# Late query projections inside the pair visit, one PSUM bank for the first product, and matmuls on zeros at the start

## The chip, the cores and the metric

The kernel runs on one core of a Trainium2 chip. The metric is the device time of one execution in microseconds (us). The kernel before takes 1054.83 us, the median of three runs (1054.11 to 1055.69).

## What is computed

Two stages follow each other. The first is linear attention over 8 batches and 8 heads (576 tokens, head dimension 64) with a feature map of 2 x 128 features; the second is a two-layer network with a squared Relu over all 4608 tokens (512 to 2048 to 512).

```python
def phi(x):
    proj = np.einsum('bhsd,df->bhsf', x, w_phi)
    proj = proj - np.max(np.abs(proj), axis=-1, keepdims=True)
    return np.concatenate([np.exp(proj), np.exp(-proj)], axis=-1)
q_p, k_p = (phi(q), phi(k))
kv = np.einsum('bhsf,bhsd->bhfd', k_p, v)
z = np.sum(k_p, axis=2)
num = np.einsum('bhsf,bhfd->bhsd', q_p, kv)
den = np.einsum('bhsf,bhf->bhs', q_p, z)[..., None] + 1e-06
attn = num / den            # heads are joined to tokens of 512 values
g = np.maximum(attn @ w_in, 0.0) ** 2
out = g @ w_out
```

## The kernel before

**Attention** goes by pairs of heads, 32 in all. The first six (`early`, L646) run step by step while the weights of the second stage are fetched and prepared. The other 26 are late pairs, and most of their matmuls stand in a *visit* (`visit`, L837): one TensorE step that holds, in this order, the key projections of pair i+1 (`k_main`, L579, in row halves of the array, and `k_tail`, L585, in column halves), the value products of pair i (L635, L640) and the numerators of pair i-1 (L853), both in column halves. The query projection of pair i is a step of its own in `late` (L920 to L926): four matmuls of 288 columns, two per head, in row halves. Its results go from three PSUM tiles to the tile `pt` by three copies (L927 to L931), and from there through a reduction over partitions on POOL (L936), a subtraction and two exponentials to the numerators of the next visit and to the denominators.

**The second stage** (`moe`, L984) goes by chunks of 256 tokens (18) and groups of 256 hidden units (8), 144 units in all. A *first product* (`gemm1`, L1002) is 24 matmuls of 256 columns into one tile `ph`; its result is split on the way to the *second product* (`gemm2`, L1032, 12 matmuls of 512 columns): Relu into `r` (L1011), its square in two precisions, `gh` (L1013) and back into `ph` (L1015), and their difference `gl` (L1018, recorded at L306).

**PSUM** has eight banks: `pp` two, `pn` and `pv` one each, `ph` two buffers of one bank, `po` two. In the first five pairs `ph` also holds the query projections (L689) and `po` the key projections.

**The order** of all instructions is written by a planner in the kernel file (`Plan.order`, L151). Each step has engines it may run on, an expected time, the steps it follows, the buffers it uses and a rank; the planner goes through time and gives each free engine the ready step of the lowest rank. Between steps of different array tilings (`mode`) it adds CHANGE to TensorE's time and prefers to stay in a tiling (STAY). The ranks of the steps up to about rank 70 come from a long string, RANKS. The order is fixed when the kernel is built; on the chip each engine takes its instructions in that order.

```python
o = P.add("PE", 1.0, q_proj, [q_load[p]], [("q", p)] + pq, R(RQ), mode=ROWS)          # L926
v = P.add("PE", us, work, after, use, rank, mode=(ROWS if k is not None else COLS, COLS))   # L871
```

Of the kernel before, what the change touches and what calls it, by code (L numbers as in the profile page):

```python
# [52 lines left out]
CHANGE = 0.15  # L53
RA, RQ, RZ = 1.3, 0.4, 0.3
COLD = 1.1
# [23 lines left out]
class Plan:  # L79
# [71 lines left out]
    def order(self):  # L151
# [36 lines left out]
        while done < len(self.ops):  # L188
# [28 lines left out]
            op.start, op.end = t, t + us * (COLD if e == "PE" and t < 125.0 else 1.0)  # L217
# [75 lines left out]
def tile_kernel(ctx, tc, qp, kp, vp, w_phi, w_in, w_out, out):  # L293
# [72 lines left out]
    ph_ = tiles(ps, "ph", [128, 2, T], F32, 2)  # L366
# [8 lines left out]
    make_identity(nc, ident)  # L375
    V.memset(ones, 1.0)
# [13 lines left out]
    def power(src, dst, top, after, uses, rank, k=1):  # L390
# [21 lines left out]
        return P.add("DVE", 0.7 + 0.16 * k, bits, [a], key + [("pn", ("pw", n))], rank)  # L412

# [104 lines left out]
    def value_in(f, n, rank, joined, pw):  # L518
# [5 lines left out]
                      for E_, us, E, lk in (("DVE", 0.64, V, 4.0), ("POOL", 1.15, G, 0.0))])  # L524
# [121 lines left out]
    def early(p):  # L646
# [42 lines left out]
        q_to = lambda h: flat(ph_[2 * p + h]) if free else pp_["qt", p][:, h, :]  # L689
        q_use = [("ph", 2 * p + h) if free else ("pp", ("qt", p)) for h in range(2)]  # L690
# [144 lines left out]
    N0 = 320  # L835

    def visit(i):  # L837
        n, s, k = (x if EARLY <= x < NPAIR else None for x in (i - 1, i, i + 1))
        rank = PER_PAIR * i + RA
        pp, pn, pv = ("pp", ("a", i)), ("pn", ("a", i)), ("pv", ("a", i))  # L840

        def work():
            if k is not None:
                k_main(k, lambda h: pp_["a", i][:, h, :])
                k_tail(k, pn_["a", i][:, N0:N0 + 128])
            if s is not None:
                kv_main(s, pv_["a", i])
                kv_tail(s, pv_["a", i])
            if n is not None:
                for to, lo, hi in ((pn_["a", i][:, 0:N0], 0, N0), (pv_["a", i][:, 256:256 + S - N0], N0, S)):  # L850
                    for s_ in range(2):
                        for h in range(2):
                            PE.matmul(out=to[64 * h:64 * h + 64, :], lhsT=kz_[n][:, 128 * s_ + 64 * h:128 * s_ + 64 * h + 64],  # L853
                                      rhs=qe_[2 * n + h].rearrange("p (s x) -> p s x", s=2)[:, s_, lo:hi],
                                      start=s_ == 0, stop=s_ == 1)

        us, after, use = 0.1, [], [pn, pv]
        if k is not None:
            loads(k, rank - 4.0)
            us += 1.24  # L860
            after += [k_load[k]]
            use += [pp, ("k", k)]
        if s is not None:
            us += 2.15
            after += exps[s] + [exp_t[s], v_load[s]]
            use += kv_use(s)
        if n is not None:
            us += 1.93
            after += [kz_of[n]] + qexp[n]
            use += [("kz", n), ("qe", 2 * n), ("qe", 2 * n + 1)]  # L870
        v = P.add("PE", us, work, after, use, rank, mode=(ROWS if k is not None else COLS, COLS))  # L871
        nums = []
        if n is not None:
            for bank, key, x, lo, hi in ((pn_, pn, 0, 0, N0), (pv_, pv, 256, N0, S)):
                first, second = copy(hi - lo, lambda lo=lo, hi=hi: n_[n][:, lo:hi],
                                     lambda bank=bank, x=x, lo=lo, hi=hi: bank["a", i][:, x:x + hi - lo])
                nums.append(P.add(*first, [v], [key, ("n", n)], rank + 0.1, other=[second]))
        if s is not None:
            turn(s, v, pv, lambda: pv_["a", i][:, 0:256], rank + 0.1)
        if k is not None:  # L880
            keys(k, v, lambda h: pp_["a", i][:, h, :], [pp, pp], v, lambda: pn_["a", i][:, N0:N0 + 128], pn, rank + 0.2)
        if n is not None:
            tokens(n, nums, rank + 0.4)
# [14 lines left out]
    def late(p):  # L898
# [17 lines left out]
        zc = P.add("DVE", 1.75, column, [o], [("z4", p), ("za", p), ("zr", p), ("zc", p)], R(RZ), lock=4.0)  # L916
        pq = [("pp", ("Q", p)), ("pn", ("Q", p)), ("pv", ("Q", p))]
        rest = lambda h: (pn_, pv_)[h]["Q", p][:, 0:SH]

        def q_proj():  # L920
            for lo in (0, SH):
                for h in range(2):
                    PE.matmul(out=rest(h) if lo else pp_["Q", p][:, h, 0:SH], lhsT=wst[64 * h:64 * h + 64, :],  # L923
                              rhs=q_[p][64 * h:64 * h + 64, lo:lo + SH], start=True, stop=True)

        o = P.add("PE", 1.0, q_proj, [q_load[p]], [("q", p)] + pq, R(RQ), mode=ROWS)  # L926
        first, second = copy(2 * SH, lambda: pt_[p][:, :, 0:SH], lambda: pp_["Q", p][:, :, 0:SH])  # L927
        pt = [P.add(*first, [o], [pq[0], ("pt", p)], R(RQ + 0.1), other=[second])]
        for h in range(2):
            first, second = copy(SH, lambda h=h: pt_[p][:, h, SH:S], lambda h=h: rest(h))  # L930
            pt.append(P.add(*first, [o], [pq[1 + h], ("pt", p)], R(RQ + 0.1), other=[second]))  # L931
        qexp[p], dens = [], []
        for h in range(2):
# [4 lines left out]
                [pt[0], pt[1 + h], pool_next], [("pt", p), ("mx", n)], R(RQ + 0.2), lock=0.0)  # L938
# [45 lines left out]
    def moe(c, f, w_done):  # L984
        n = c * NFP + f
        m, bank = LEAD + n, n + 2 * BANKS
# [20 lines left out]
        if f:  # L1007
# [4 lines left out]
            out=r_[n], in_=ph_[bank], func=AF.Relu, scale=cw[:, f, 0:1]), [g1], [("ph", bank), ("r", n)], Q)  # L1012
        sq = P.add("ACT", act_us(512), lambda: A.activation(out=gh_[n], in_=r_[n], func=AF.Square),  # L1013
                   [o], [("r", n), ("gh", n)], Q)
        o = P.add("ACT", 0.59, lambda: A.activation(out=ph_[bank], in_=r_[n], func=AF.Square),  # L1015
                  [o], [("ph", bank), ("r", n)], Q, other=[("DVE", 0.76, lambda: V.scalar_tensor_tensor(
                      out=ph_[bank], in0=ph_[bank], scalar=cw[:, f, 0:1], in1=r_[n], op0=ALU.mult, op1=ALU.mult), None)])
        o = P.add("DVE", 0.70, lambda: sub(V, gl_[n], ph_[bank], gh_[n].bitcast(F32)),  # L1018
                  [o, sq], [("ph", bank), ("gh", n), ("gl", n)], Q)
# [15 lines left out]
        g2 = P.add("PE", 2.74, gemm2, [o] + list(w_done[f, False]),  # L1035
# [93 lines left out]
    "ACD]1k>%<ELlWgVP]lB._^StESJfL=[CY1ITMeI#4rABQDZ$UqY(KKZeKGZnL{PDPuM2OLG#M&E$Z8LYVwTQJYT.?SO_MMe0ND?a"  # L1129
    "N@WsXNNtERMlHBMtHkO6L*ZtGSHYJHNhR-W<B>HtLuQ@KqViKUHdM<J1B5S3OMU>Q/Qe]DJwJ?Qy_1AgGsR{Z^AVU}RgU-7fI_B3"  # L1130
    "D7P=NZBcA!7HV=Ny@bHWO[K0E$W1D/JrFc:,RXC*_xV<]|NEUk?2S,DyP`;?SsLM@d@mQQGBJ@K8E0QFQ)AJM#g@L=>OUOMbHzJj"
    "J@NOM6M=SbPIOQJ#>pKC6iKzIMDSLtJOH,KJ:UQ#ORVXAjVOM&SLV$4YTFDoC8>KNI>>GoE0Wm@HA)JOK/QX?*[sXqIYE2EfLr^1"
    "TXTIA4A=fIF1DDPXPk/dOjK=W|L=AfM:EKC=<ADTH/EHDrJ[A.IEQJCeS+<.WPVuL;GJX0ZeNvOsEhJ?Q;J*E)LlK?KqGnE=G=^/"
    "D{LQ:3EN?pPT_C1QNZ<QTdEG;QOzD)P8=RM^ASM3MbHoa=HMNnG.7oD|Q7^JVBL}T5QpNJMKBnGGNEE.2G@PX<LHIYH!P(Q4B%=O"
# [50 lines left out]
```

## Time and profile before

| What | Value |
|---|---|
| median of 3 runs | 1054.83 us |
| the profiled execution | 1055.12 us |
| its span, first to last instruction | 1053.3 us |
| mean granted TensorE clock | 0.994 of 2.4 GHz |
| instructions | 19429 |
| busy: TensorE (PE) / VectorE (DVE) / ScalarE (ACT) / GpSimd (POOL) | 1025.4 / 718.4 / 620.4 / 164.6 us |
| HBM read and written | 59.18 and 12.99 MB |

All rows come from one profiled execution; its times count from the span's start. PE is TensorE's matmuls, PEld its weight loads, which overlap them. The matmuls are pipelined and a row's duration runs into the next row, so the time that a step takes on TensorE is read from its start to the start of what follows. An engine's idle time stands in brackets behind a row, with what released it.

### The profile page before, as it was taken

Reading aid. Unit: us, or ns where it says so; the run is one execution under the profiler, and the core shown is the slowest. Engines: PE = TensorE matmul, PEld = TensorE weight load, DVE = VectorE, ACT = ScalarE, POOL = GpSimd, SP = SyncE. Lnnn points to the kernel's source line nnn. Section 1 sums busy time; section 2 is a strip of 40 time slices with the busy share of each in tenths; the row PEclk is TensorE's granted clock in tenths of the full one; section 3 lists DMA queues with packets and bytes.
Section 4 is the critical chain, followed back from the end, with each engine's and each line's share of the span. In section 5 each row is a group of like instructions: output and inputs, shape, how many; then the busy total and the mean of one; then the engine's idle time right before and its main releaser. Section 6 shows DMA issues by size and latency. Waiting matters only on the chain.

```text
span 1053.3 us, 19429 instructions
## 1 busy us (share of the span) xinstructions
PE 1025.4 (97%) x7678; PEld 706.6 (67%) x7762; DVE 718.4 (68%) x1526; ACT 620.4 (59%) x1117; POOL 164.6 (16%) x86
## 2 busy tenths in 40 slices
PE   8869999999999999999999999999999999999998
PEld 6545766667767666666676666676666666677775
DVE  5877688887897887878787767787687775111111
ACT  7896875666665555666666655566555555333333
POOL 2532411111110111111111011111110111000000
PEclk9998999999999999999999999999999999999999
DMA  9834222212222120222221221122121101000000
GB/s 356 299 122 148 100 68 77 77 47 68 77 58 74 50 72 20 74 58 77 58 77 58 57 78 44 41 55 73 45 65 27 45 16 43 1 21 21 1 21 21
DMA packets 66143, 73.47 MB, mean 70 GB/s; under 512 B 35204, under 2 KB 44036, under 8 KB 64004
## 3 DMA queue, kind: packets, MB, share of 16 engines
q1 hardware_dynamic: 66052, 72.22, 21.8%
q8 instruction: 61, 1.00, 0.4%
q14 instruction: 30, 0.25, 0.1%
HBM read 59.18 MB, written 12.99 MB: 69 GB/s over the span
## 4 chain that ended last, share of the span: by engine, by line
PE 93%; DMA 3%; ACT 2%; DVE 1%; issue 1%; SPq 0%; ACTq 0%; DVEq 0%
PE po L1032 37%; PE ph L1002 36%; PE pv L635 5%; PE pp L579 3%; PE pn L853 3%; PE pv L853 2%; PE pp L923 2%; DMA raw0o<-in_w_out_dram 1%; PE pn L923 1%; PE pv L640 1%; PE pn L585 1%; DMA k<-in_kp_dram 1%; PE pv L749 1%; PE pn L398 0%; PE pp L730 0%
## 5 line engine op out<-in xcount | busy, mean ns | idle before, releaser
L1002 PE MATMUL ph<-ring,win 128*128 128x256 f16 x3456 | 400.6, 273 | 0.0
L1002 PEld LDWEIGHTS <-win 128*128 128x128 f16 x3456 | 336.3, 98 | 72.0 <-issue 10.2
L1011 ACT ACTIVATE r<-ph,cw 128x512 f32<-128x512 f32 x144 | 99.1, 688 | 248.1 <-PE ph L1002 247.7
L306 DVE TENSOR_TENSOR gl<-ph,gh 128x512 bf16<-128x512 f32 x144 | 98.9, 686 | 183.9 <-ACT ph L1015 178.1
L936 POOL PARTITION_ALL_REDUCE mx<-pt x52 | 114.3, 2198 | 635.7 <-ACT pt L310 420.0
L1032 PE MATMUL po<-wh,gh 128*128 128x512 f32 x576 | 172.5, 420 | 0.0
L1032 PE MATMUL po<-wl,gl 128*128 128x512 bf16 x560 | 147.0, 379 | 0.8
L1032 PE MATMUL po<-wl,gh 128*128 128x512 bf16 x508 | 135.1, 381 | 4.6
L1032 PEld LDWEIGHTS po<-wh,gh 128*128 128x128 f32 x576 | 99.0, 189 | 29.1 <-issue 9.8
L1032 PEld LDWEIGHTS <-gl 128*128 128x128 bf16 x576 | 56.3, 98 | 68.0
L1013 ACT ACTIVATE gh<-r 128x512 fp32r<-128x512 f32 x144 | 90.9, 631 | 5.8 <-PE po L1032 1.6
L1032 PEld LDWEIGHTS <-gh 128*128 128x128 bf16 x576 | 44.8, 98 | 73.5 <-issue 39.8
L1015 ACT ACTIVATE ph<-r 128x512 f32<-128x512 f32 x144 | 84.4, 586 | 0.5
L635 PE MATMUL pv<-e,v 128*64 128x256 f32 x512 | 63.5, 391 | 0.6 <-ACT kz L310 0.4
L310 ACT ACTIVATE n<-pn 128x320 f32<-128x320 f32 (+1 forms) x32 | 13.8, 431 | 77.4 <-PE pn L853 77.1
L950 DVE SCALAR_TENSOR_TENSOR pt<-qe,zc,pt 128x576 f32<-128x576 f32 x52 | 42.3, 816 | 19.3 <-ACT pt L948 18.8
L306 DVE TENSOR_TENSOR qe<-pt,mx 128x576 f32<-128x576 f32 x52 | 39.0, 750 | 17.1 <-POOL mx L936 16.8
L601 ACT ACTIVATE e<-e 128x512 f32<-128x512 f32 x64 | 39.8, 622 | 17.2 <-DVE e L598 17.2
L941 ACT ACTIVATE qe<-qe 128x576 f32<-128x576 f32 x52 | 35.1, 675 | 22.4 <-DVE qe L306 22.4
L635 PEld LDWEIGHTS pv<-e,v 128*64 128x64 f32 x512 | 37.2, 141 | 16.3 <-issue 2.3
L887 DVE STREAM_TRANSPOSE kvs<-pv 128x256 f32<-128x256 f32 x26 | 11.5, 444 | 48.8 <-PE pv L853 44.6
L948 ACT ACTIVATE pt<-qe,zc 128x576 f32<-128x576 f32 x52 | 40.2, 775 | 3.9
(188 smaller groups left out, 1281.2 us busy)
## 6 DMA issues: line engine op xcount, KB each, us to landing
v<-in_vp_dram SPq DMA_DIRECT2D x32, 320.0 KB
k<-in_kp_dram SPq DMA_DIRECT2D x32, 288.0 KB
q<-in_qp_dram SPq DMA_DIRECT2D x32, 288.0 KB
rb<-rd SPq DMA_DIRECT2D x64, 144.0 KB
out_dram<-o SPq DMA_DIRECT2D x34, 256.0 KB
td<-kvs SPq DMA_DIRECT2D x26, 128.0 KB
kz<-td SPq DMA_DIRECT2D x104, 32.0 KB
raw0i<-in_w_in_dram SPq DMA_DIRECT2D x1, 1024.0 KB
```

Source lines behind the costliest of these rows:

```text
L306: eng.tensor_tensor(out=out_, in0=a, in1=b_, op=ALU.subtract)
L601: o = P.add("ACT", act_us(512), lambda n=n: A.activation(out=e_[n][:, :, 1, :], in_=e_[n][:, :, 0, :], func=AF.Exp, scale=-1.0), [o], [("e ...
L635: PE.matmul(out=to[64 * h:64 * h + 64, 0:256], lhsT=v_[p][:, t, h, :], rhs=e_[2 * p + h][:, t].rearrange("p s f -> p (s f)"), start=t == 0 ...
L853: PE.matmul(out=to[64 * h:64 * h + 64, :], lhsT=kz_[n][:, 128 * s_ + 64 * h:128 * s_ + 64 * h + 64], rhs=qe_[2 * n + h].rearrange("p (s x) ...
L936: o = P.add("POOL", par_us(S), lambda n=n, h=h: G.partition_all_reduce(mx_[n], pt_[p][:, h, :], channels=128, reduce_op=bass_isa.ReduceOp. ...
L948: o = P.add("ACT", act_us(S, 1), lambda h=h, qe=qe, y=y: A.activation(out=y(), in_=qe(0), func=AF.Copy, scale=zc_[p][:, 2 * h:2 * h + 1]), ...
L950: o = P.add("DVE", 0.82, lambda h=h, qe=qe, y=y: V.scalar_tensor_tensor(out=y(), in0=qe(1), scalar=zc_[p][:, 2 * h + 1:2 * h + 2], in1=y() ...
L1002: PE.matmul(out=ph[:, j, :], lhsT=win[w][:, t, 128 * ff:128 * ff + 128], rhs=ring[half][x][:, t, c0:c0 + T], start=k == 0, stop=k == 3 * K ...
L1011: o = P.add("ACT", act_us(512, 1), lambda: A.activation(out=r_[n], in_=ph_[bank], func=AF.Relu, scale=cw[:, f, 0:1]), [g1], [("ph", bank), ...
L1013: sq = P.add("ACT", act_us(512), lambda: A.activation(out=gh_[n], in_=r_[n], func=AF.Square), [o], [("r", n), ("gh", n)], Q)
L1015: o = P.add("ACT", 0.59, lambda: A.activation(out=ph_[bank], in_=r_[n], func=AF.Square), [o], [("ph", bank), ("r", n)], Q, other=[("DVE", ...
L1032: PE.matmul(out=po_[po[i][1]], lhsT=g[:, j, 128 * i:128 * i + 128], rhs=w[:, j, :], start=(ff == 0 and s == 0), stop=(ff == 2 * NFP - 1 an ...
```

## The change

- The query projection of a late pair is no step of its own any more. The visit has three steps: *rows* (512 columns of both heads' query projections into `pn` and `pv`, then the keys), *columns* (the last 64 query columns, the keys' tail, the value products, all into a new one-bank tile `pz`) and *numerators* into `pn` and `pv`, which wait for the copies of the query projections out of these banks. The copies are of 512, 512 and 2 x 64 columns.
- `ph` has one buffer instead of two; its bank goes to `pz`. In the first five pairs the query projections use `ph` and `pz`.
- r squared is kept in `r` in SBUF. The second square runs in place behind `gh` on ScalarE or VectorE, and `gl` reads `r` and `gh`. The Relu may also run on VectorE.
- At the start TensorE runs eight matmuls of 512 columns on a tile of zeros.
- The scaling of the input weights may no longer run on POOL.
- The planner's numbers: CHANGE is 0.18 instead of 0.15, a slower TensorE ahead of 125 us is no longer assumed, a step that holds a single bank already is not released by that bank's last use, and RANKS is another string.

```diff
-CHANGE = 0.15
+CHANGE = 0.18
-COLD = 1.1
+WARM = 8
...
-            least = max([open_at.get(tag, 0.0) for tag, n in alone(op)] + [a.start + 0.001 for a in op.behind], default=0.0)
+            least = max([open_at.get(tag, 0.0) for tag, n in alone(op) if holder.get(tag) != n] + [a.start + 0.001 for a in op.behind], default=0.0)
...
+    pz_ = tiles(ps, "pz", [128, 512], F32, 1, None)
-    ph_ = tiles(ps, "ph", [128, 2, T], F32, 2)
+    ph_ = tiles(ps, "ph", [128, 2, T], F32, 1)
...
+    warmer = o_[0].bitcast(BF16)[:, 0:512]
+    V.memset(warmer, 0.0)
...
+    def warm():
+        for _ in range(WARM):
+            PE.matmul(out=pn_["warm", 0], lhsT=warmer[:, 0:128], rhs=warmer, start=True, stop=True)
+    P.add("PE", 3.2, warm, [], [("pn", ("warm", 0))], -100.0)
...
-                      for E_, us, E, lk in (("DVE", 0.64, V, 4.0), ("POOL", 1.15, G, 0.0))])
+                      for E_, us, E, lk in (("DVE", 0.64, V, 4.0),)])
...
+        def rows():
+            if s is not None:
+                for h in range(2):
+                    PE.matmul(out=(pn_, pv_)[h]["Q", i], lhsT=wst[64 * h:64 * h + 64, :], rhs=q_[s][64 * h:64 * h + 64, 0:512],
+                              start=True, stop=True)
             if k is not None:
                 k_main(k, lambda h: pp_["a", i][:, h, :])
...
+        def columns():
+            for h in range(2 if s is not None else 0):
+                for c in range(0, 128, 64):
+                    PE.matmul(out=pz_["a", i][c:c + 64, 64 * h:64 * h + 64], lhsT=wbf[:, 128 * h + c:128 * h + c + 64],
+                              rhs=q_[s][:, 512:576], start=True, stop=True)
+            if k is not None:
+                k_tail(k, pz_["a", i][:, 128:256])
             if s is not None:
+                kv_main(s, pz_["a", i][:, 256:512])
+                kv_tail(s, pz_["a", i][:, 256:512])
...
+            v = P.add("PE", us_r, rows, need, use_r, R(0.0), mode=ROWS)
+            c = P.add("PE", us_c, columns, need + [v], use_c, R(0.0), mode=COLS)
...
+            v3 = P.add("PE", 1.94, numerators, need + [c] + pt_of.get(s, [])[:2], use_n, R(0.0), mode=COLS)
...
-        o = P.add("PE", 1.0, q_proj, [q_load[p]], [("q", p)] + pq, R(RQ), mode=ROWS)
...
-        o = P.add("ACT", 0.59, lambda: A.activation(out=ph_[bank], in_=r_[n], func=AF.Square),
-                  [o], [("ph", bank), ("r", n)], Q, other=[("DVE", 0.76, lambda: V.scalar_tensor_tensor(
...
-        o = P.add("DVE", 0.70, lambda: sub(V, gl_[n], ph_[bank], gh_[n].bitcast(F32)),
-                  [o, sq], [("ph", bank), ("gh", n), ("gl", n)], Q)
+        o = P.add("ACT", act_us(512), lambda: A.activation(out=r_[n], in_=r_[n], func=AF.Square),
+                  [sq], [("r", n)], Q, other=[("DVE", 0.70, lambda: V.tensor_tensor(
+                      out=r_[n], in0=r_[n], in1=r_[n], op=ALU.mult), 4.0)])
+        o = P.add("DVE", 0.70, lambda: sub(V, gl_[n], r_[n], gh_[n].bitcast(F32)),
+                  [o, sq], [("r", n), ("gh", n), ("gl", n)], Q, lock=4.0)
```

## Rows read from the trace of the kernel before

**Rows 1.** The page's first part: busy us, share of the span, instructions.
```profile
PE 1025.4 (97%) x7678; PEld 706.6 (67%) x7762; DVE 718.4 (68%) x1526; ACT 620.4 (59%) x1117; POOL 164.6 (16%) x86
```

**Rows 2.** Stretches: busy us of PE, PEld, DVE, ACT, POOL; granted clock, DMA, GB/s.
```profile
0.00:125.00 125.00, 106.03 (x1071) 74.12 (x1074) 90.84 (x162) 101.58 (x178) 45.41 (x33) 0.96 0.60 216
...
50.00:75.00 25.00, 20.92 (x256) 13.28 (x254) 19.57 (x39) 23.70 (x42) 9.83 (x5) 1.00 0.45 138
500.00:600.00 100.00, 99.35 (x733) 67.80 (x742) 78.17 (x174) 61.49 (x114) 12.85 (x6) 1.00 0.23 64
```

**Rows 3.** TensorE's time line around one query projection: start us, us, instruction.
```profile
480.91 2.78 PE L1002 MATMUL ph<-ring,win 128*128 128x256 f16 x24
483.62 0.76 PE L923 MATMUL pp<-q,wraw 64*128 64x288 f32 x4
...
484.79 1.20 PE L1032 MATMUL po<-wh,gh 128*128 128x512 f32 x4
...
487.57 2.78 PE L1002 MATMUL ph<-ring,win 128*128 128x256 f16 x24
490.11 1.18 PE L1032 MATMUL po<-wh,gh 128*128 128x512 f32 x4
...
492.86 0.39 PE L398 MATMUL pn<-ident,m 128*128 128x128 f32 x2
```

**Rows 4.** TensorE's time line through one visit.
```profile
501.10 1.16 PE L579 MATMUL pp<-wraw,k 64*128 64x128 f32 x16
502.19 0.44 PE L585 MATMUL pn<-wraw,k 128*64 128x128 f32 x4
502.46 1.90 PE L635 MATMUL pv<-e,v 128*64 128x256 f32 x16
504.18 0.60 PE L640 MATMUL pv<-et,v 128*64 128x256 f32 x4
504.61 1.25 PE L853 MATMUL pn<-qe,kz 128*64 128x320 f32 x8
...
506.65 1.20 PE L1032 MATMUL po<-wh,gh 128*128 128x512 f32 x4
```

**Rows 5.** The time lines of ScalarE and VectorE during that visit.
```profile
501.20 0.69 ACT L1011 ACTIVATE r<-ph,cw 128x512 f32<-128x512 f32 x1 [1.98 <-PE ph L1002]
501.92 0.63 ACT L1013 ACTIVATE gh<-r 128x512 fp32r<-128x512 f32 x1
502.46 0.58 ACT L1015 ACTIVATE ph<-r 128x512 f32<-128x512 f32 x1
...
503.68 0.64 DVE L306 TENSOR_TENSOR gl<-ph,gh 128x512 bf16<-128x512 f32 x1
```

**Rows 6.** Single lines of the kernel: duration in ns, shortest, median and longest.
```profile
L617 DVE TENSOR_TENSOR ez<-e x52: 635/688/1660, 135.1 to 844.8; 128x512 f32<-128x512 f32 x52
...
L306 DVE TENSOR_TENSOR gl<-ph,gh x144: 640/692/693, 100.2 to 1046.2; 128x512 bf16<-128x512 f32 x144
...
L936 POOL PARTITION_ALL_REDUCE mx<-pt x52: 2141/2142/2689, 143.8 to 877.8; - x52
...
L310 ACT ACTIVATE pt<-pp x26: 628/632/652, 142.7 to 873.7; 128x576 f32<-128x576 f32 x26
```

**Rows 7.** The head: TensorE's time line, and the stretch from 79 to 86 us.
```profile
4.18 0.69 PE L585 MATMUL pn<-wraw,k 128*64 128x128 f32 x4 [4.18 <-DMA k<-in_kp_dram]
4.80 2.08 PE L579 MATMUL po<-wraw,k 64*128 64x128 f32 x16
...
35.25 1.16 PE L579 MATMUL po<-wraw,k 64*128 64x128 f32 x16 [1.84 <-DMA k<-in_kp_dram]
...
79.30 1.09 PE L730 MATMUL pp<-ident,pt 128*128 128x128 f32 x4 [4.88 <-DVE e L598]
...
80.84 3.68 PE L635 MATMUL pv<-e,v 128*64 128x256 f32 x16 [0.16 <-ACT n L310]
...
79.00:86.00 7.00, 6.54 (x30) 3.94 (x32) 5.11 (x7) 5.61 (x10) 2.02 (x1) 0.51 0.43 148
```

More of the change, by code (lines that the diff above doesn't have):

```diff
@@ L216, in order @@
             us, _, lock = op.ways[e]
-            op.start, op.end = t, t + us * (COLD if e == "PE" and t < 125.0 else 1.0)
+            op.start, op.end = t, t + us
             if lock is not None:
@@ L835, in tile_kernel @@
     N0 = 320
+    pt_of = {}
     def visit(i):
@@ new lines, in numerators @@
+        def numerators():
+            for to, lo, hi in ((pn_["n", i][:, 0:N0], 0, N0), (pv_["n", i][:, 0:S - N0], N0, S)):
+                for s_ in range(2):
+                    for h in range(2):
+                        PE.matmul(out=to[64 * h:64 * h + 64, :], lhsT=kz_[n][:, 128 * s_ + 64 * h:128 * s_ + 64 * h + 64],
+                                  rhs=qe_[2 * n + h].rearrange("p (s x) -> p s x", s=2)[:, s_, lo:hi],
+                                  start=s_ == 0, stop=s_ == 1)
+        us_r, us_c, need, use_r, use_c, use_n = 0.0, 0.0, [], [pz], [pz], [pn, pv]
@@ L858, in visit @@
         if k is not None:
             loads(k, rank - 4.0)
-            us += 1.24
-            after += [k_load[k]]
-            use += [pp, ("k", k)]
-        if s is not None:
-            us += 2.15
-            after += exps[s] + [exp_t[s], v_load[s]]
-            use += kv_use(s)
-        if n is not None:
[L868 to L871, printed above, removed]
+            us_r += 0.9
@@ new lines, in visit @@
+        if us_r:
+            v = P.add("PE", us_r, rows, need, use_r, R(0.0), mode=ROWS)
+            c = P.add("PE", us_c, columns, need + [v], use_c, R(0.0), mode=COLS)
+        if s is not None:
+            pt_of[s] = []
+            for h, (to, key) in enumerate(((pn_, qn), (pv_, qv))):
+                first, second = copy(512, lambda h=h: pt_[s][:, h, 0:512], lambda to=to: to["Q", i])
+                pt_of[s].append(P.add(*first, [v], [key, ("pt", s)], R(0.05), other=[second]))
+            first, second = copy(128, lambda: pt_[s][:, :, 512:576],
+                                 lambda: pz_["a", i][:, 0:128].rearrange("p (h x) -> p h x", h=2))
+            pt_of[s].append(P.add(*first, [c], [pz, ("pt", s)], R(0.05), other=[second]))
@@ L872, in visit @@
         nums = []
         if n is not None:
-            for bank, key, x, lo, hi in ((pn_, pn, 0, 0, N0), (pv_, pv, 256, N0, S)):
+            v3 = P.add("PE", 1.94, numerators, need + [c] + pt_of.get(s, [])[:2], use_n, R(0.0), mode=COLS)
+            for bank, key, lo, hi in ((pn_, pn, 0, N0), (pv_, pv, N0, S)):
                 first, second = copy(hi - lo, lambda lo=lo, hi=hi: n_[n][:, lo:hi],
-                                     lambda bank=bank, x=x, lo=lo, hi=hi: bank["a", i][:, x:x + hi - lo])
-                nums.append(P.add(*first, [v], [key, ("n", n)], rank + 0.1, other=[second]))
+                                     lambda bank=bank, lo=lo, hi=hi: bank["n", i][:, 0:hi - lo])
+                nums.append(P.add(*first, [v3], [key, ("n", n)], R(0.1), other=[second]))
@@ L914, in column @@
                 V.tensor_copy(out=zc_[p][32 * b:32 * b + 32, :], in_=zr_[p].rearrange("p (j b) -> p b j", b=4)[:, b, :])
[L916 to L924, printed above, removed]
-        o = P.add("PE", 1.0, q_proj, [q_load[p]], [("q", p)] + pq, R(RQ), mode=ROWS)
[L927 to L931, printed above, removed]
+        zc = P.add("DVE", 1.8, column, [o], [("z4", p), ("za", p), ("zr", p), ("zc", p)], R(RZ), lock=4.0)
+        pt = pt_of[p]
         qexp[p], dens = [], []
@@ L985, in moe @@
         n = c * NFP + f
-        m, bank = LEAD + n, n + 2 * BANKS
+        m, bank = LEAD + n, n + BANKS
         half, c0 = divmod(c * T % RING, HR)
@@ L1128 @@
 RANKS = (
[L1129 to L1133, printed above, removed]
```

87 lines of the change are left out of this document (48 added, 39 removed).

## The prediction, made before the kernel with the change was run

> **What bounds the kernel now.** I read the page's engine table first, then three stretches, then TensorE's own time line. TensorE is busy for 97% of the span, and in the steady part for more: 99.35 of 100 us between 500 and 600, against 78 on VectorE and 61 on ScalarE [rows 1, 2]. There a microsecond of TensorE work is a microsecond of the run, and an instruction elsewhere is free until its queue is late. The first 125 us are of another kind: TensorE idles 19 of them, and from 50 to 75 ScalarE is the fuller engine with 23.70 of 25 [rows 2]. So the steady part is costed by TensorE's columns, the head by what its waits could give back.
>
> **The unit of the steady part** is a first product and a second product. From 487.57 to 490.11 a first product takes 2.54 us, from there to 492.86 a second one 2.75, together 5.29 [rows 3]. What lies between such pairs is attention.
>
> **What is removed: the query projection as a step of its own.** There are 26 late pairs, each with its projection at line 923, and every one has products on both sides: 14 times a first product ahead and a second behind, 12 times another order. From 480.91 to 487.57 (first product, projection, second product) 6.66 us go by where 5.29 would without it: 1.37 us [rows 3]. The projection itself is 1.17 of that (483.62 to 484.79), the other 0.20 is what its neighbours lose by the change of tiling. The 12 in another order lie between 1.17 and 1.37; one neighbour pays in each, so 1.30. Weighted, 1.34 us per pair are removed, 34.8 in all.
>
> **What is added to the visit.** The row half holds 512 columns per head, both heads at once on the two row halves, in two passes, as every float32 matmul here. The price of a column comes from the value products: eight instructions of 256 columns per column half last from 502.46 to 504.18, 0.215 each [rows 4]. So 512 columns last 0.43 and two passes 0.86. The visit opens in this tiling anyway, for the keys, so no change of tiling comes with it. The column half holds the last 64 columns: four instructions per column half (two heads, two passes), 0.21 by columns alone. But short instructions cost more than their columns: the keys' 16, eight per row half, last from 501.10 to 502.19, 0.136 each for 128 columns worth 0.107, and line 585's, two per column half, last 0.27 [rows 4]. If 0.136 is a floor per instruction, four cost 0.54. The nearest reading is 0.03 on top of the columns, so 4 x (0.053 + 0.03) = 0.33; I take that and keep 0.21 and 0.54 as ends. Added: 0.86 + 0.33 = 1.19. Net 1.34 - 1.19 = 0.15 per pair, times 26 **3.9 us gained**. The ends: 1.34 - 1.07 gives 7.0 gained, 1.30 - 1.40 gives 2.6 lost.
>
> **The new wait inside the visit.** The numerators now write the two banks that the projection filled, and so wait for two copies of 512 columns, each under the 0.632 of the copy of 576 [rows 6]. The projection's matmuls end 0.9 us after the visit opens. ScalarE is then busy with the Relu and the two squares of the product before, until 503.04, 1.94 after the opening [rows 5]; with two copies behind that it is 3.2. Meanwhile TensorE has the keys, the 64 columns, the keys' tail and the value products: 0.86 + 1.09 + 0.33 + 0.27 + 1.72 + 0.43 = 4.7 us [rows 4]. With 1.5 to spare the wait costs nothing; without that cover TensorE stands still or the planner puts a product in between (rival b). Behind the numerators only products are queued. The copies hold the same 1152 columns per pair, so ScalarE's sum stays. The query load on SP goes out when the projection two pairs earlier frees its buffer, a whole pair ahead of its use; being needed at the visit takes less than half of that away, and nothing on SP moves behind it.
>
> **One bank for the first product.** A product can start only when the Relu of the one before has read the bank. In the visit shown the Relu starts 0.10 us behind its product and takes 0.69 [rows 4, 5]: the bank is free after 0.8, and a second product of 2.75 mostly stands in between, 1.95 more than needed. I cost it at nothing; the cover is gone once ScalarE comes to the Relu over 1.95 late (rival c). Two first products in direct succession must be pulled apart: 0.8 each if kept, nothing if reordered.
>
> **r squared in SBUF.** The second square writes SBUF, which puts it between 0.58 (it now) and 0.63 (the square that writes gh) [rows 5]. The subtraction gl takes 0.692 in the median with its square in PSUM; the sum at line 617, with both operands in SBUF, 0.688 [rows 6]. gl is done at 504.32, and the next second product starts at 506.65 [rows 4, 5]: 2.3 us of cover, and gl is its last third. So nothing again. What the move exposes stands in the maxima: 1.660 for line 617, 0.693 for gl in 144 [rows 6].
> The Trainium skill ("SBUF — State Buffer", Who interferes with whom) has a rule against this: a VectorE instruction with two SBUF inputs contends with a GpSimd instruction that reads SBUF, and the later one fully blocks. The maximum of line 617 agrees.
> Whatever stretches line 617 can stretch gl now. POOL is busy for 164.6 us, 16% of the span [rows 1]; 16% of 144 are 23 subtractions, and half a reduction of 2.14 [rows 6] makes 25 us on VectorE and under 2.2 on any gl. The sum takes nothing for it; what it does if VectorE cannot absorb it is rival d.
>
> **The head.** Eight matmuls of 512 16-bit columns: a first product has 24 of 256 in 2.54 us [rows 3], so 0.21 each, or 0.42 at half the clock, 3.4 us in all. TensorE has nothing to do until the first keys at 4.18 [rows 7], so the zeros end near there, perhaps 0.5 after. The 16 key matmuls at 4.80 then take 2.08 us where 16 take 1.16 at 35.25 [rows 7]: half rate, the 1.2 GHz level. At the full level the matmuls up to 8.9 would end some 1.9 earlier, and as much again may come from the next group. But TensorE is not what fills this part, and the next keys have to land. Between a loss of 0.5 and a gain of 3 I take 1. The new priorities set the head in another order. Today it holds a stall of 4.88 at 79.30, for VectorE's e, and after it a clock granted at 0.51 until 86, with value products of 3.68 for 1.90 [rows 4, 7]: 4.9 + half of 6.5, or 8 us. An order without that gives up to 8, one with another such stall loses as much. ScalarE's fullness sets the first tokens, so I take 2.
>
> **Sum.** The profiled execution took 1055.12 us (span 1053.3 and 1.8 around it), 0.3 above the median of 1054.83. 1055.1 - 3.9 - 1 - 2 = 1048.2, as a median **1047.9 us**. A measurement of this kernel can tell about 0.2%, 2.1 us, from no change.
>
> **Rivals.**
> (a) The head loses its stall and low clock altogether: 1055.1 - 3.9 - 3 - 8 = 1040, with the cheap end of the columns 1037. For: TensorE idles 19 us ahead of 125. Against: ScalarE is full there. Chance 0.15.
> (b) The numerators are parted from the columns. Another change of tiling costs the 0.20 seen around the projection, and a start of their own 0.1; 0.15 gained turns into 0.15 lost, 3.9 us, and with the head's 3 the time is 1056. For: ScalarE can hold the copies back. Against: 1.5 us to spare. Chance 0.14.
> (c) Slower: the single bank. Its place is every first product of the steady part. A Relu queued behind three ScalarE instructions of 0.63 starts 1.9 late and stops TensorE. It decides from a mean wait of 0.05 us (6.9 over 144 products); one in three waiting 0.3 is 14 us, so 1062. For: ScalarE is 61% busy, and a second bank covers it today. Against: 0.10 behind its product is how the Relu starts now, and VectorE may take it. Chance 0.12.
> (d) Two SBUF inputs: 25 us more on a VectorE at 78% delay the key chain, one visit in two by a microsecond: 1060. Chance 0.06.
> (e) The zeros do not do what they say, and the clock is still low when the keys come: 0.5 late and no gain, 1049.4. Chance 0.07.
> The forecast as told has 0.46, with 1041 to 1053 by the ends of its own terms.
>
> **Range and chances.** 1038 to 1058 leaves out a part of (a) and most of (c) and (d), 0.2 together. Faster by over 2.1 us are the forecast but for its edge, (a), most of (e) and a little of (b): 0.70. Within it lies most of (b): 0.11. Slower are (c), (d) and the rest of (b): 0.19.
>
> **What would show it.** No projection between two products; a visit of 5.55 + 1.19 = 6.7 us with rows, columns and numerators in one piece, 0.33 of it for the last 64 query columns; no Relu among TensorE's waits; gl with a median of 0.69 and single ones up to 2 us; the first keys' matmuls in 1.2 rather than 2.08. I am wrong if the numerators stand alone, if products wait for the Relu, or if the gain lies in the first 125 us alone.

## The result and the profile after

| | before | after |
|---|---|---|
| median, us | 1054.83 | 1046.92 |
| its executions | 1052.91 to 1055.69 (5) | 1042.14 to 1047.77 (5) |
| the profiled execution, span | 1055.12, 1053.3 | 1042.14, 1040.4 |

The ratio is 0.9919, with the interval 0.9894 to 0.9945: 7.9 us faster, 1.0 below the predicted 1047.9 and inside the range. The profiled execution of after is the fastest of its five, 4.8 below their median, so its total can't be set against that of before as it stands.

The page of after, span and first part, answers to [rows 1]:

```profile
span 1040.4 us, 19694 instructions
...
PE 1021.0 (98%) x7874; PEld 701.0 (67%) x7874; DVE 735.0 (71%) x1525; ACT 639.6 (61%) x1118; POOL 169.0 (16%) x87
```

VectorE and ScalarE have 17 and 19 us more to do than in [rows 1]; TensorE has 4 less and is still the bound. The stretches of after, with the columns of [rows 2], and one more from the head:

```profile
10.00:20.00 10.00, 10.00 (x117) 7.45 (x117) 8.39 (x17) 9.38 (x22) 2.72 (x2) 0.84 1.02 418
0.00:125.00 125.00, 109.35 (x1129) 73.55 (x1130) 99.06 (x179) 103.06 (x181) 42.51 (x32) 0.99 0.61 219
50.00:75.00 25.00, 19.26 (x218) 12.03 (x210) 21.14 (x38) 20.98 (x41) 8.85 (x5) 1.00 0.53 170
500.00:600.00 100.00, 100.00 (x748) 69.05 (x746) 78.89 (x171) 63.54 (x113) 13.67 (x6) 1.00 0.19 56
```

Between 500 and 600 TensorE shows no gap where it showed 0.65 us before, but that is no gain to count: the same kernel, run again with the same time for the whole part, shows 99.45 there with 740 matmul records instead of 748. Ahead of 125 it idles 15.7 us instead of 19, and ScalarE is less full from 50 to 75 (20.98 for 23.70). TensorE's time line in after: the start, the first product, one visit with its neighbours, the end:

```profile
1.17 3.60 PE L419 MATMUL pn<-o 128*128 128x512 bf16 x8 [1.17 <-DVE o L378]
4.70 1.94 PE L588 MATMUL po<-wraw,k 64*128 64x128 f32 x16
...
9.79 2.17 PE L588 MATMUL po<-wraw,k 64*128 64x128 f32 x16 [1.69 <-DMA k<-in_kp_dram]
...
90.72 2.79 PE L1026 MATMUL ph<-ring,win 128*128 128x256 f16 x24
...
477.63 2.78 PE L1026 MATMUL ph<-ring,win 128*128 128x256 f16 x24
480.17 1.18 PE L1058 MATMUL po<-wh,gh 128*128 128x512 f32 x4
...
483.02 0.69 PE L856 MATMUL pn<-q,wraw 64*128 64x512 f32 x1
...
483.98 1.06 PE L588 MATMUL pp<-wraw,k 64*128 64x128 f32 x16
484.97 0.45 PE L864 MATMUL pz<-q,wraw 128*64 128x64 f32 x8
485.25 0.39 PE L594 MATMUL pz<-wraw,k 128*64 128x128 f32 x4
485.47 1.90 PE L644 MATMUL pz<-e,v 128*64 128x256 f32 x16
487.20 0.60 PE L649 MATMUL pz<-et,v 128*64 128x256 f32 x4
487.63 1.25 PE L876 MATMUL pn<-qe,kz 128*64 128x320 f32 x8
488.71 1.03 PE L876 MATMUL pv<-qe,kz 128*64 128x256 f32 x8
489.67 2.79 PE L1026 MATMUL ph<-ring,win 128*128 128x256 f16 x24
...
1031.04 1.18 PE L1058 MATMUL po<-wh,gh 128*128 128x512 f32 x4
```

The visit runs in one piece from 483.02 to 489.67: 6.65 us where that of [rows 4] took 5.55. The query rows take 0.96, the keys 0.99, the 64 columns 0.28, the keys' tail 0.22; the value products take 1.73 and 0.43 as in [rows 4], the numerators 2.04. ScalarE's time line in that visit, with the copies for which the numerators wait:

```profile
484.18 0.60 ACT L310 ACTIVATE pt<-pn 128x512 f32<-128x512 f32 x1 [1.71 <-PE pv L856]
484.67 0.59 ACT L310 ACTIVATE pt<-pv 128x512 f32<-128x512 f32 x1
```

They end at 485.26, and the numerators start at 487.63: 2.4 us to spare. Single lines of after, in the columns of [rows 6]:

```profile
L306 DVE TENSOR_TENSOR gl<-r,gh x144: 636/693/2861, 95.6 to 1033.4; 128x512 bf16<-128x512 f32 x144
...
L626 DVE TENSOR_TENSOR ez<-e x52: 636/687/2860, 96.2 to 830.5; 128x512 f32<-128x512 f32 x52
```

The waits of TensorE in after, the longest first (total us, times, longest); no other in the list is above 1.5, and none is for a Relu:

```profile
PE po L588 <- DMA k<-in_kp_dram: 3.2, 2, 1.7
PE pv L644 <- ACT kz L310: 1.5, 3, 0.7
PE ph L705 <- DVE pt L718: 1.5, 1, 1.5
```

**Where the time went.** Three points on TensorE's time line split each execution: the start of the first product (until there is the head), the start of the last group of second products, and the end, 9.3 us behind that in both kernels.

| | first product | last group | between |
|---|---|---|---|
| before | 94.89 | 1044.02 | 949.13 |
| after | 90.72 | 1031.04 | 940.32 |

8.8 us came out of the part from the first product on, and 4.2 out of the head. The fastest execution flatters the head: if the later part lasts as long in the median execution of after (span 1045.1), its first product starts near 95.5, later than in before. No execution of 1047 of this kernel was traced, but two close relatives below were, at 1047.71 (eight more matmuls on zeros) and 1048.11 (filled pauses): 940.32 in both, first products at 96.27 and 96.69.

The two parts do not hold quite the same work. The keys of the seventh pair stand behind the first product in before, and ahead of it in after, on TensorE's time lines of before and after:

```profile
94.89 3.38 PE L1002 MATMUL ph<-ring,win 128*128 128x256 f16 x24
...
129.93 1.16 PE L579 MATMUL pp<-wraw,k 64*128 64x128 f32 x16
```

```profile
85.64 1.16 PE L588 MATMUL pp<-wraw,k 64*128 64x128 f32 x16 [0.48 <-DVE pt L718]
```

With their tail they take 1.2 us in a visit of after. So 1.2 of the 8.8 crossed the split and is not saved; like for like the later part gives 7.6. That the gain of the median lies there and not in the head was put to the test.

By kinds, TensorE's time from the first product on changed so, each kind counted from its start to the next one's: products 766.9 to 761.5; query projections, keys and keys' tails 65.9 to 62.7, of which 1.2 is the pair that moved; the rest by 0.2. Of the 5.4 on the products, 0.6 is the first one of before, which ran at a low clock (the row of 3.38 us, where others take 2.78).

### The profile page after: what moved, and what is told of

Read it like the earlier page. It is cut to its first block, busy times and chain, and to the rows that moved or that the text cites. A ratio compares the mean times of both kernels' runs of the same rounds, so it can differ in the third digit from the quotient of the medians.

```text
span 1040.4 us, 19694 instructions
## 1 busy us (share of the span) xinstructions
PE 1021.0 (98%) x7874; PEld 701.0 (67%) x7874; DVE 735.0 (71%) x1525; ACT 639.6 (61%) x1118; POOL 169.0 (16%) x87
## 4 chain that ended last, share of the span: by engine, by line
PE 94%; ACT 2%; DMA 2%; DVE 1%; SPq 0%; issue 0%; ACTq 0%
PE po L1058 37%; PE ph L1026 36%; PE pz L644 4%; PE pn L876 3%; PE pn L856 3%; PE pp L588 2%; PE pv L876 2%; DMA k<-in_kp_dram 2%; PE pz L649 1%; PE pz L864 1%; PE pv L644 1%; PE pz L594 1%; PE pn L758 0%; PE pn L775 0%; PE pp L739 0%; PE pv L677 0%
## 5 line engine op out<-in xcount | busy, mean ns | idle before, releaser
L306 DVE TENSOR_TENSOR gl<-r,gh 128x512 bf16<-128x512 f32 x144 | 102.2, 709 | 193.7 <-ACT r L1041 192.9
L960 POOL PARTITION_ALL_REDUCE mx<-pt x52 | 119.8, 2303 | 604.2 <-ACT pt L310 557.5
L1058 PE MATMUL po<-wh,gh 128*128 128x512 f32 x576 | 170.3, 416 | 0.0
L1058 PE MATMUL po<-wl,gh 128*128 128x512 bf16 x576 | 149.6, 382 | 0.0
L1041 ACT ACTIVATE r<-r 128x512 f32<-128x512 f32 x144 | 90.7, 630 | 4.6
L610 ACT ACTIVATE e<-e 128x512 f32<-128x512 f32 x64 | 40.0, 626 | 35.7 <-DVE e L607 35.5
L604 DVE TENSOR_REDUCE km<-pp 128x4 f32<-128x512 f32 x54 | 36.6, 684 | 30.1 <-PE pp L588 30.0
L626 DVE TENSOR_TENSOR ez<-e 128x512 f32<-128x512 f32 x52 | 45.8, 880 | 5.1 <-ACT e L612 4.6
L644 PE MATMUL pz<-e,v 128*64 128x256 f32 x416 | 49.3, 379 | 0.0
L612 ACT ACTIVATE e<-e 128x512 f32<-128x512 f32 x64 | 40.2, 628 | 1.4
L978 DVE STREAM_TRANSPOSE yt<-pt 128x576 f32<-128x576 f32 x52 | 40.3, 774 | 0.8
```

The source lines that it names most:

```text
L306: eng.tensor_tensor(out=out_, in0=a, in1=b_, op=ALU.subtract)
L626: o = P.add("DVE", dve_us(512), lambda n=n: V.tensor_tensor(out=ez_[n].rearrange("p t x -> p (t x)"), in0=e_[n][:, 0:2].rearrange("p t s f ...
L644: PE.matmul(out=to[64 * h:64 * h + 64, 0:256], lhsT=v_[p][:, t, h, :], rhs=e_[2 * p + h][:, t].rearrange("p s f -> p (s f)"), start=t == 0 ...
L960: o = P.add("POOL", par_us(S), lambda n=n, h=h: G.partition_all_reduce(mx_[n], pt_[p][:, h, :], channels=128, reduce_op=bass_isa.ReduceOp. ...
L978: o = P.add("DVE", dve_us(S), lambda n=n, y=y: V.transpose(yt_["y", n - 2 * EARLY], y()), [o], [("pt", p), ("yt", ("y", n - 2 * EARLY))], ...
L1041: o = P.add("ACT", act_us(512), lambda: A.activation(out=r_[n], in_=r_[n], func=AF.Square), [sq], [("r", n)], Q, other=[("DVE", 0.70, lamb ...
```

## The experiments

**The changed kernel again**, for its spread.

> The changed kernel once more, to see whether its single executions spread by the clock of the head. Theory V (the visit): the stretch from the first product to the end takes 949 to 950 us in any execution, 8 to 9 less than before, and what differs between executions (1042 to 1048) lies ahead of it, with a lower mean granted clock. Rival H (the head): the stretch from the first product is as long as before, 958, in an execution of 1047, and only the head has become shorter.

Median 1046.37 (1043.2 to 1050.99) against 1054.4, ratio 0.9924 [0.9902, 0.9946]. The first product starts at 92.56, and from there to the last group 940.31 us pass, 0.01 from the table above. Later it ran once more beside other kernels:

> The changed kernel as the base of the two runs beside it: a median of 1045 to 1047, single executions from 1042 to 1051, the longer ones with the lower mean granted clock (0.998 to 0.990).

1045.25 (1043.66 to 1047.49), 0.9915 [0.9897, 0.9933]; first product at 93.14, then 940.32. The 17 executions of the changed kernel lie 8.9 us apart, and a shorter time goes with a higher mean clock: 0.998 up to 1043.7, 0.993 from 1046.9 on but for one, the longest, at 0.990. The three that were traced are all on the shorter side, and differ in the head alone. In [rows 7] a low clock stood at 79 to 86; here it stands early: between 10 and 20 in after (0.84 above), and in the first repetition so:

```profile
12.00:16.00 4.00, 3.04 (x15) 1.72 (x17) 3.93 (x7) 3.94 (x10) 1.15 (x1) 0.50 1.04 429
16.00:20.00 4.00, 4.00 (x50) 2.75 (x50) 0.93 (x4) 1.64 (x4) 1.28 (x2) 0.66 1.01 416
```

**The zeros, taken away from the changed kernel.**

```diff
     def warm():
-        for _ in range(WARM):
-            PE.matmul(out=pn_["warm", 0], lhsT=warmer[:, 0:128], rhs=warmer, start=True, stop=True)
+        pass
```

> The changed kernel without the eight matmuls on zeros, all else in the same order. If they are worth what I took for them, it is 1 us slower than the changed kernel (0 to 1.5). Rival: the clock that they raise carries through the head, then it is 3 us slower or more and the mean granted clock is lower. Second rival: they delay the first keys for nothing, then it is 0.5 us faster.

1044.84 (1042.5 to 1046.96), 0.9906 [0.9891, 0.9921]: no slower than with the zeros. **The zeros, put alone into the kernel before**, its order unchanged:

```diff
 make_identity(nc, ident)
+warmer = o_[0].bitcast(BF16)[:, 0:512]
+V.memset(warmer, 0.0)
+for _ in range(8):
+    PE.matmul(out=pn_["warm", 0], lhsT=warmer[:, 0:128], rhs=warmer, start=True, stop=True)
```

> The kernel before with the eight matmuls on zeros put in front, its order else unchanged. Theory: no change that can be told, 1052.5 to 1055.5, since ScalarE and the DMA set the head from 10 us on. Rival: the zeros are a part of the gain by themselves, then 1051 or less.

1055.05 against 1054.4, 1.0003 [0.9994, 1.0013]: nothing. The key matmuls of the first two pairs tell why, on TensorE's time line, first without zeros (changed kernel), then with them (the second repetition):

```profile
4.10 2.08 PE L587 MATMUL po<-wraw,k 64*128 64x128 f32 x16 [4.10 <-DMA k<-in_kp_dram]
...
9.45 2.17 PE L587 MATMUL po<-wraw,k 64*128 64x128 f32 x16 [0.50 <-DMA k<-in_kp_dram]
```

```profile
4.70 1.24 PE L588 MATMUL po<-wraw,k 64*128 64x128 f32 x16
...
10.08 1.25 PE L588 MATMUL po<-wraw,k 64*128 64x128 f32 x16 [2.24 <-DMA k<-in_kp_dram]
```

With zeros the first keys start 0.6 later and run at the full rate (1.24 where 2.08), so they end some 0.2 sooner. The second pair's keys then wait for their load in both, 2.24 instead of 0.50, start 0.6 later and end 0.3 sooner. In this execution the zeros do what the change says, in after hardly (1.94); most of what they win is waited away.

**The square of r in SBUF, alone in the kernel before**, order unchanged. Here r's place isn't held until `gl` has read it, so `gl` is formed from other values in units where the place is used again first; instructions and shapes are those of the change.

```diff
-            lambda: A.activation(out=ph_[bank], in_=r_[n], func=AF.Square)
+            lambda: A.activation(out=r_[n], in_=r_[n], func=AF.Square)
...
-            lambda: sub(V, gl_[n], ph_[bank], gh_[n].bitcast(F32))
+            lambda: sub(V, gl_[n], r_[n], gh_[n].bitcast(F32))
```

> The kernel before with r squared in SBUF and nothing else; its order was planned without it. Theory: within 1 us of before (1053.8 to 1055.8), gl 0.69 in the median with a maximum of 1.5 to 2.8 where it meets POOL, and no wait of TensorE for gl. Rival d: gl and the key chain come late, TensorE waits for gl or for keys, 1058 or more.

1053.68 against 1054.4, 0.9994 [0.9985, 1.0003]: nothing. The single line of `gl`:

```profile
L306 DVE TENSOR_TENSOR gl<-r,gh x144: 635/693/2872, 98.1 to 1044.1; 128x512 bf16<-128x512 f32 x144
```

The place alone makes the longest 2.872 where it was 0.693 in [rows 6], and leaves the median. 16 of the 144 last over 1 us, most of them 1.2 to 1.4, and each of the 16 starts while a POOL instruction runs (13 times the reduction over partitions). No wait of TensorE is for `gl`. What stands beside a long one is seen in after, which has two (1.32 and this one), on the time lines of VectorE and POOL:

```profile
134.84 2.86 DVE L306 TENSOR_TENSOR gl<-r,gh 128x512 bf16<-128x512 f32 x1
```

```profile
131.62 5.54 POOL L306 TENSOR_TENSOR wl<-u,wh 128x1024 bf16<-128x1024 f32 x2 [5.00 <-DVE u L466]
```

`gl` begins inside POOL's two subtractions on the split weights and ends 0.5 us behind them (137.70 and 137.16). In after the long ones are mostly elsewhere: 11 of the 52 sums at line 626 last over 1 us, all beside POOL, where before has one; these sums take 45.8 us in all for 36.6.

**The order without the string of ranks**, in both kernels: the ranks stay as the steps were given them.

```diff
             i, j = (DIGITS.index(x) for x in RANKS[2 * n:2 * n + 2])
-            op.rank = (90 * i + j - 3000) * 0.05
+            pass
```

> The kernel before with the string of ranks left unread, so that the planner orders by the ranks that the code gives. It is the base for the next run; slower than before by some 10 to 40 us, mostly in the head. Its query projections stand alone, 26 of them, as before.

> The changed kernel with its string of ranks left unread. Theory V (the visit gives the gain, in any order): faster than the kernel before without its string by 5 to 9 us, and in its trace the visits are 6.6 us long where the numerators follow directly. Rival S (the new string gives the gain): within 2 us of it, or slower.

Before without its string: 1058.08 against 1053.49, 1.0048 [1.003, 1.0065]. Changed without its string: 1060.86, 1.0066 [1.0053, 1.0079]. On the time line:

| | first product | from it to the last group |
|---|---|---|
| before, no string | 100.81 | 949.93 |
| changed, no string | 108.28 | 941.43 |

Neither expectation came out whole. The later part has its gain without any string, 8.5 us (some 7 like for like, since the seventh pair's keys crossed the split here too). The head loses 7.5 in these executions. That of before is the longest of its four (1061.86), so by the medians, with the later parts as in the table, the head loses 11.3. So the changed kernel as a whole is slower than the one before. What it waits for there, in the list of TensorE's waits:

```profile
PE pp L739 <- DVE e L607: 7.6, 1, 7.6
...
PE pp L739 <- DVE pt L718: 3.1, 1, 3.1
...
PE ph L1026 <- ACT r L1035: 1.6, 2, 0.8
```

The stall of [rows 7] for VectorE's `e` is back, longer (7.6 for 4.88), and two products wait for the Relu of the one before. The granted clock is lower there as well: 0.70 from 75 to 100 and 0.84 from 100 to 125, where the kernel before without its string has 0.84 and 1.00. How the loss divides between waits and clock was not isolated. The new string brings the head back to where the old one had it in the kernel before.

**Numerators parted from the columns.** In all 25 visits that have both, the next product is moved ahead of the numerators; nothing else is changed.

```diff
+        ops = P.improve()
+        for num in [op for op in ops if op.fn.__name__ == "numerators"]:
+            i = ops.index(num)
+            j = next(j for j in range(i + 1, len(ops)) if ops[j].fn.__name__ in ("gemm1", "gemm2"))
...
+                ops.insert(i, ops.pop(j))
```

> The changed kernel with the next product moved ahead of the numerators in all 25 visits in which they stood behind the value products; nothing else is moved. Theory: a change of tiling and a start of their own, 0.2 to 0.3 us each, so 5 to 7.5 us slower than the changed kernel, 1051 to 1054: what the joining gave is gone. Rival: the numerators cost the same wherever they stand, then within 1.5 us of the changed kernel.

1054.45 (1052.03 to 1058.1) against 1053.49, 1.0005 [0.9992, 1.0018]; from the first product to the last group 949.73, 9.4 longer than in the changed kernel. One parted visit on the time line:

```profile
495.98 0.60 PE L649 MATMUL pz<-et,v 128*64 128x256 f32 x4
496.51 2.79 PE L1026 MATMUL ph<-ring,win 128*128 128x256 f16 x24
499.24 1.30 PE L876 MATMUL pn<-qe,kz 128*64 128x320 f32 x8
500.37 1.03 PE L876 MATMUL pv<-qe,kz 128*64 128x256 f32 x8
501.33 1.20 PE L1058 MATMUL po<-wh,gh 128*128 128x512 f32 x4
```

Nothing waits here. The value products' last group takes 0.53 for 0.43, the product 2.73 for 2.54, the numerators 2.09 for 2.04: 0.34 in this visit. In all 14 visits where a first product was moved in between it is 0.35, in the 11 with a second product 0.25: 7.7 us of the 9.4. The other 1.7 is at five places elsewhere in the order, where a product lasts 0.2 to 0.8 longer; at 452.59 a first product waits 0.60 for the Relu. So a piece in its own tiling between two products costs 0.31 on average beside its columns. The kernel before had its numerators joined too; what this order undoes is therefore not what the change gained, and that the sums are alike is chance. It prices a parted piece, as the query projection was one.

**Second products put ahead of the visit.** In 11 visits that are entered from a first product, the second product that follows the visit goes ahead of it.

```diff
...
+            if name(before) == "gemm1" and name(ops[j]) == "gemm2" and all(at[id(a)] < i for a in ops[j].after + ops[j].behind):
+                ops.insert(i, ops.pop(j))
```

> The changed kernel with 11 visits put one second product later, so that 21 of them instead of 11 are entered from a second product and left to a first one; nothing else is moved. In the trace of the changed kernel a first product ahead of a visit takes 2.71 instead of 2.54 and a second product behind it 2.78 instead of 2.75, against 2.85 and 2.55 in the other order: 0.20 against 0.11 per visit. Theory: the stretch from the first product to the last group of matmuls, 940.3 us in every execution of the changed kernel, gets 1.0 shorter, 939.3; the median goes down by as much, which the spread of the head (1042 to 1051) can hide. Rival: the attention behind the visit is late by a product and TensorE waits for it somewhere, then the stretch is 941 or longer.

1051.9 (1048.51 to 1054.8) against 1054.11, 0.9976 [0.9964, 0.9987]; the part between the points is 946.44, 6.1 longer than in the changed kernel. This is the rival's case. A wait of TensorE heads its list that the list of after doesn't have:

```profile
PE ph L1026 <- ACT r L1035: 3.2, 7, 1.0
```

One of the seven, on the time lines of TensorE and ScalarE:

```profile
444.69 2.79 PE L1026 MATMUL ph<-ring,win 128*128 128x256 f16 x24
447.24 1.18 PE L1058 MATMUL po<-wh,gh 128*128 128x512 f32 x4
...
450.48 2.78 PE L1026 MATMUL ph<-ring,win 128*128 128x256 f16 x24 [0.32 <-ACT r L1035]
```

```profile
447.35 0.63 ACT L610 ACTIVATE e<-e 128x512 f32<-128x512 f32 x1 [2.14 <-DVE e L607]
448.02 0.63 ACT L612 ACTIVATE e<-e 128x512 f32<-128x512 f32 x1
...
449.10 0.76 ACT L829 ACTIVATE ring<-rb,cb 128x576 f16<-128x576 f32 x1
449.76 0.67 ACT L1035 ACTIVATE r<-ph,cw 128x512 f32<-128x512 f32 x1
```

The product ends at 447.24, its Relu starts 2.5 later behind exponentials and a scaling, and the next first product stands. By kinds the loss stands at the second products, 392.3 to 398.7 us, since each kind runs to the start of the next. The 3.2 is idle time alone. A wait also costs the overlap with the row behind it: from 447.24 to 450.48 a second product lasts 3.24 where others take 2.75, and the seven that stand ahead of these waits last 4.3 longer in all. Two second products wait for an output copy on VectorE, which the list of after doesn't have either (1.0 us idle, 1.5 in all), and five more products last 0.2 to 0.3 longer, 1.2 together. Against these 7.0 the new entries give back the 1.0 that the theory said, near enough to the 6.1 measured.

**More zeros and filled pauses**, to see whether a steady clock in the head gives its spread back. First eight more matmuls on zeros ahead of the second pair's keys:

```diff
...
+            if p == 1:
+                for _ in range(8):
+                    PE.matmul(out=pp_["warm", 0][:, 0, :], lhsT=warmer[:, 0:128], rhs=warmer, start=True, stop=True)
+            k_main(p, k_to)
```

> The changed kernel with eight more matmuls on zeros ahead of the second pair's keys, where TensorE stands idle from about 8 to 9.8 us and the following matmuls run at half rate until about 13.5. Theory: with that pause filled the clock stays up from about 6.5 us on, no low clock in the profile up to 20 us, and the median is 1 to 3 us under the changed kernel's 1046.4, with less spread. Rival: the clock there is not on the path, then within 1 us; or the zeros delay the second keys, then slower by up to 1.

1044.78 (1042.92 to 1047.71), 0.9916 [0.9901, 0.9931]. The granted clock is 1.00 from 0 to 50, and the time lies within the changed kernel's own spread: the low clock just moves, to 0.91 from 50 to 75 and 0.89 from 75 to 100. Then 17 matmuls on zeros in seven pauses that the planner foresees between 55 and 95, and both together:

```diff
...
+                if 55.0 < last < 95.0 and pause > 0.4:
...
+                    for _ in range(min(6, int(pause / 0.3))):
+                        PE.matmul(out=to, lhsT=warmer[:, 0:128], rhs=warmer, start=True, stop=True)
```

> The changed kernel with matmuls on zeros in TensorE's planned pauses between 55 and 95 us (17 matmuls of 512 columns in 7 places), the order else unchanged. Theory C (the clock of the head makes the spread, and it falls after those pauses): no low clock between 55 and 95 in the profile, a median of 1042 to 1044, 2 to 4 us under the control, and a narrower spread. Rival A (ScalarE and VectorE set the first tokens, whatever the clock): the clock is up, but the median is within 1 us of the control. Second rival: the zeros hold TensorE up where its pause is shorter than planned, 1 us or more slower.

> As the run before, and eight more matmuls on zeros ahead of the second pair's keys. Theory C: low clock only ahead of about 6.5 us, a median of 1041.5 to 1043. Rival A: within 1 us of the control.

Filled pauses: 1048.08 (1047.76 to 1049.17), 0.9939 [0.9926, 0.9953], 2.8 above the changed kernel beside it; the spread is narrower, at its long end. Both: 1046.86, 0.9931 [0.9916, 0.9947]. Neither beats the changed kernel. With both, the granted clock of the traced execution is 0.93 from 25 to 50 and 1.00 in the other quarters of the first 100 us, and still the first product starts at 95.34, later than in any trace of the changed kernel. So a nearly steady clock, bought this way, doesn't bring the head forward. The filling itself comes late, on TensorE's time line of the first of the two:

```profile
58.73 0.61 PE L1158 MATMUL pn<-o 128*128 128x512 bf16 x1 [0.73 <-DVE n L311]
...
61.40 2.19 PE L758 MATMUL pv<-qe,kz 128*64 128x288 f32 x8
```

The zeros wait for a bank that VectorE is still reading, and what follows runs at a low clock (2.19; eight such matmuls take 1.19 at 89.60 in after). No version tried beats the changed kernel by more than its spread.

## Why the prediction was right, and where its terms were not

The direction, the bound and the place of the gain held; the median came within 1.0 us. That closeness is luck in part, since two terms were off and cancel: the steady part was put at 3.9 and gave 7.0, and all else was put at 3 and gave 0.9 in the median (the keys that moved into the head and the cold first product counted there). Point by point:

- **What is removed**, 1.34 per pair. The projections themselves took 1.17 (30.5 us over 26); the products lost (5.45 - 0.59) / 26 = 0.19 to them, where the prediction had 0.17. Together 1.36. Right.
- **What is added, 1.19 per pair, is the mis-sized term.** The row half came out to the hundredth: 0.96 + 0.99 = 1.95, where the prediction had 0.86 + 1.09. The column half did not: the 64 columns took 0.28 for 0.33, and the keys' tail behind them, where it is no longer the first of its tiling, 0.22 for 0.27. That is 1.09 in the visit shown. Over all pairs the query projections, keys and tails together took 2.0 us less (the 3.2 above without the 1.2 of the pair that crossed the split), 0.08 per pair where the prediction had 0.02 more. With the 4.9 on the products that is 6.9 us, 0.26 per pair where the prediction had 0.15, and close to its own end of 7.0. With the 0.2 of the rest the steady part gave 7.0.
- **The numerators joined.** The order with them parted costs 0.31 per visit, so the price in rival (b), 0.20 + 0.1, was right. Its total of 1056 compares with the 1054.45 measured for what it describes, which holds 1.7 us of other waits. What kept (b) from happening is the cover for the copies, 2.4 us where 1.5 was predicted. How the 0.31 divides between leaving and entering a tiling was not isolated.
- **One bank for the first product**, at nothing: right, with no Relu in TensorE's waits. It is right for this order only. Moving 11 second products is enough to bring in the wait of rival (c), seven times, 3.2 us idle and 4.3 in all, so its mechanism is real, though smaller than the 6.9 at which (c) would decide, and far from the 14 that it priced; the "mostly a second product in between" of the prediction is something that the order has to keep.
- **r squared in SBUF**, at nothing: right (0.9994 alone). Single `gl` reach 2.86 where the prediction said up to 2. Rival (d) counted 23 long ones; there are 16 with this edit alone (11.4 us more) and two in after, 2.8 us more on an engine that has 21% to spare, where (d) had 25. The prediction did not ask how the new order would place the sums of line 626 (617 before); with their 9.2 it is 12 us in after, and TensorE idles for none of it in the steady part. The rule of the Trainium skill ("SBUF — State Buffer", Who interferes with whom) agrees with the rows in that both `gl` and POOL's subtraction read SBUF and `gl` ends just behind it.
- **ScalarE's sum** was to stay. Added up over its instructions it grew by 6.2 us, as much as the second square alone (0.630 on average where it took 0.586, 144 times); the copies stayed (37.4 and 37.9). The page's busy time grew by 19.2 because it counts overlapping rows once, and they overlap less in after. At 64 of 100 us it costs nothing in this order.
- **The zeros, 1 us: failed.** The first keys reach the full rate in some executions (1.24), as said, and not in all (1.94 in after). The clause "the next keys have to land" was most of the answer: the gain ends in a DMA wait. Rival (e) names another cause for much the same time.
- **The new order, 2 us: failed in the median.** Without the strings the change costs the head 11.3 us by the medians (7.5 in the traces), so the new string makes up for the change rather than adding to it. The 4.2 that the profiled execution shows ahead of the first product is the fast end of a spread. Rival (a), 1040, is what the luckiest executions come near (1042.14).

What stays open: what sets where in the head the clock falls, what the executions of 1047 and more do there, since none of the changed kernel's was traced, and whether an order exists that takes the head to rival (a) every time. The planner's numbers and the scaling taken from POOL were not run alone, and no run put a projection of its own back into the changed kernel: that its removal is the gain is read from the time by kinds, in a part where TensorE is the bound, and from the price of a parted piece.

## What to carry to other kernels

Price a step that moves into a neighbour's tiling by what it costs in that place, not by its columns with a start of its own: the group that comes first is the dearer one (the keys' tail took 0.27 first in its tiling and 0.22 behind the 64 columns), and a parted group costs its neighbours as well (0.31 us here). A buffer given up costs nothing only as long as the order keeps other work between its uses, so order and buffers have to be changed together. Where a kernel has an unsteady head and a steady rest, cut the trace at the point where they meet: the rest repeated to 0.02 us here, while totals spread over 9 us and one profiled execution would have put a third of the gain (4.2 of 13.0) in the wrong place. Then compare the work on both sides of that point: one pair's keys crossed it here, 1.2 us that look like a gain and are none.

## What the runs showed of the hardware

- The order of instructions is fixed, yet the stretch of low granted clock falls elsewhere with small edits of the head: between 10 and 19 us in the changed kernel's traces, 70 to 75 (0.66) in the one without zeros, and the time of one kernel moves by up to 8.9 us along with its mean clock. From the first product on the duration repeats within 0.02 us.
- Matmuls on zeros that run from 1.17 at 0.42 us each are followed by keys at the full rate in one execution (1.24) and at nearly half of it in another (1.94), with the same instructions ahead.
- The longest VectorE subtraction of 512 columns went from 0.693 to 2.872 us when one of its inputs moved from PSUM to SBUF, while its median stayed at 0.693; each of the 16 over 1 us started while a POOL instruction ran.
- Products last longer ahead of a group in another tiling: in the changed kernel a first product takes 2.71 us ahead of a visit and 2.54 ahead of a second product, a second product 2.85 ahead of a visit and 2.75 ahead of a first product.
